# Spreading weight conversions over 19 steps, a longer output lag and one product on GpSimd, in a fused attention and gated MLP kernel

## The chip, the cores and the metric

The kernel runs on one core of one Trainium2 chip. The metric is the device time in microseconds, lower is better.

## The reference, cut to what matters

```python
# x: (8, 8, 512, 64), state: (8, 8, 32, 64); w_in: (512, 2048), w_out: (2048, 512), both float64
a  = softmax(scale * x @ state.T);  xread = a @ state        # tokens read the states
a2 = softmax(scale * state @ x.T);  sread = a2 @ x           # states read the tokens
t  = concat([xread, sread], axis=2)  -> (4352, 512)
h  = t @ w_in
return (h * cos(h)) @ w_out
```

The weights arrive as float64 and the kernel builds float32 from their bits on the chip. That is the conversion which the change moves.

## The kernel before

The kernel is one long software pipeline. Step s computes the hidden tile s (128 hidden features by 512 tokens of one batch), gates it, and multiplies a tile of some steps ago with `w_out`. Steps 0 to 15 are batch 0, steps 16 to 31 batch 1. The two form a pair with four phases of eight tiles (steps 0-7, 8-15, 16-23, 24-31), because the product with `w_out` is done in seven in place of eight block products; the sums of blocks s1 to s4 of `w_out` are built on GpSimd in steps 15 to 23.

A float64 piece of the weights is converted in parts on three engines:

```python
    def convert_part(i, p):
        ...
        if p == "1":   nc.scalar.activation(dst, raw_high, func=ACTF.Abs)
        elif p == "2": nc.scalar.activation(e, raw_low, func=ACTF.Copy, scale=2.0 ** -51, bias=2.0)
        elif p == "a": nc.vector.tensor_scalar(dst, dst, 2.0 ** -15, None, op0=ALU.max)          # L211
        elif p == "b": nc.vector.tensor_scalar(bits, bits, 3, None, op0=ALU.logical_shift_left)  # L213
        elif p == "c": nc.vector.scalar_tensor_tensor(...)                    # the sign, L216
        else:                                                                 # "d", L222
            engine = nc.vector if i == 1 else nc.gpsimd
            engine.tensor_tensor(bits, bits, e.bitcast(I32), op=ALU.add)      # the low word
```

There are 18 pieces for this pipeline. Pieces 0 to 3 are converted ahead of it (the last two parts of piece 3 in step 0). Piece i of the rest gets "1", "2", "a" and "b" at its step in `conv_at`, and "c" and "d" one step later. The order within a step, which is the order on each engine, is this (cut):

```python
    for step, t in enumerate(tiles()):
        ...
        hidden(t)            # TensorE: 2 x matmul of sw = w_in @ state with a, into one of two PSUM buffers
        go(0)                # TensorE work of the attention: products, token transposes, scores, ...
        gate(t)              # ScalarE copy + magic constant
        gate2(t)             # VectorE subtraction (first gate instruction on VectorE)
        go(1); go(3)         # ScalarE copies; VectorE copies, maxima, sums, norm1
        if last >= 0: convert(last, "cd")
        gate3(t)             # ScalarE Abs, Sin
        gate4(t)             # VectorE product h * cos(h): frees the PSUM buffer
        if conv >= 0: convert(conv, "1")                     # ahead of gate3 where go(1) is empty
        sums(t)              # differences of g for the block products (GpSimd in the first pair)
        go(2)
        if conv >= 0: convert(conv, "2")
        go(4)
        if conv >= 0: convert(conv, "ab")
        if step in block_at: blocks(*block_at[step])         # GpSimd
        while len(line) >= (LAG if step >= NH else LAG + 1): # LAG = 3, NH = 8
            output(line.pop(0))                              # TensorE: tile x w_out, L489
        line.append(t)
```

`norm1` is the product of the unnormalised attention with the spread inverse of its sums, 128x1024 float32 with both inputs in SBUF; for batch 1 it stands in step 11.

## Time and profile before

| | before |
|---|---|
| time, median | 821.85 us |
| TensorE busy / span | 765.5 / 819.9 us |
| TensorE's waits from 58 to 140 us | 17.4 us |
| ... after 140 us | 4.3 us |
| VectorE busy from 100 to 120 us | 17.99 of 20 us |

The table is read from the page's first part, from TensorE's waits by window and from the busy times by stretch; the prediction shows those lines.

### The profile page before, as it was taken

The numbers are of one execution on the slowest core, as the hardware profiler recorded it, in microseconds if no ns is written. First come the engines' busy times: TensorE is split into PE (matmuls) and PEld (weight loads), VectorE is DVE, ScalarE is ACT, GpSimd is POOL, SyncE is SP. The second block draws the span as 40 slices with busy tenths as digits, with TensorE's granted clock in tenths as the row PEclk, the third lists the DMA queues.
The fourth block names the chain that finished last, engine by engine and source line by source line (L and its number), as shares of the span: only waits on it lengthen the run. The fifth ranks groups of instructions, "written<-read, shape, count | busy, mean of one in ns | idle before, by whom it ended". The sixth has DMA issues, their size and how long they took to land.

```text
span 819.9 us, 7479 instructions
## 1 busy us (share of the span) xinstructions
PE 765.5 (93%) x2720; PEld 345.0 (42%) x2720; DVE 434.6 (53%) x672; ACT 397.9 (49%) x644; POOL 175.6 (21%) x117
## 2 busy tenths in 40 slices
PE   3569688989999999999999999999999999999997
PEld 2133233434444444444444444444344444455554
DVE  2799897653355435863454456743554355432431
ACT  2568675564447344644455454634473445322222
POOL 1134236877100000154000000451000002620200
PEclk9999999999999999999999999999999999999999
DMA  6574450102000211030010311120000112200021
GB/s 154 179 203 158 153 154 0 27 0 52 1 13 14 52 26 26 13 65 0 1 26 1 64 21 19 26 52 0 14 14 0 27 26 50 79 0 14 13 39 38
DMA packets 110500, 37.18 MB, mean 45 GB/s; under 512 B 102464, under 2 KB 102464, under 8 KB 110464
## 3 DMA queue, kind: packets, MB, share of 16 engines
q1 hardware_dynamic: 109248, 36.19, 18.8%
q10 hardware_dynamic: 1088, 0.26, 0.2%
q8 instruction: 21, 0.34, 0.2%
q0 software_dynamic: 128, 0.26, 0.2%
q14 instruction: 15, 0.12, 0.1%
HBM read 27.79 MB, written 8.91 MB: 45 GB/s over the span
## 4 chain that ended last, share of the span: by engine, by line
PE 78%; DVE 12%; ACT 7%; issue 1%; DMA 1%; POOL 0%; SPq 0%; DVEq 0%; POOLq 0%
PE o L489 42%; PE h L424 25%; PE at L276 4%; PE o L606 3%; DVE q L433 2%; PE at L363 2%; ACT q L439 1%; DVE g_all L445 1%; PE at L249 1%; ACT q L438 1%; DVE w_in L211 1%; DVE w_out L211 1%; DVE xT L296 1%; DVE aT L340 1%; DMA x_b<-in_x_dram 1%
## 5 line engine op out<-in xcount | busy, mean ns | idle before, releaser
L424 PE MATMUL h<-aT,sw 128*128 128x512 f32 x512 | 244.0, 599 | 17.9 <-DVE g_all L445 14.1
L489 PE MATMUL o<-g_all,w_out 128*128 128x512 f32 x512 | 236.5, 598 | 5.5 <-DVE sw L403 2.9
L430 ACT ACTIVATE q<-h 128x512 f32<-128x512 f32 (+1 forms) x144 | 82.2, 571 | 269.6 <-PE h L424 269.6
L451 POOL TENSOR_TENSOR g_all<-g_all 128x512 f32<-128x512 f32 x80 | 112.1, 1424 | 460.1 <-DVE g_all L445 454.5
L433 DVE SCALAR_TENSOR_TENSOR q<-q,h 128x512 f32<-128x512 f32 (+1 forms) x144 | 94.3, 655 | 208.0 <-ACT q L430 208.0
L489 PE MATMUL o<-g_all,s 128*128 128x512 f32 x384 | 177.3, 598 | 0.0
L445 DVE TENSOR_TENSOR g_all<-h,q 128x512 f32<-128x512 f32 (+1 forms) x144 | 94.8, 658 | 139.7 <-ACT q L439 139.4
L424 PEld LDWEIGHTS h<-aT,sw 128*128 128x128 f32 x512 | 96.6, 191 | 145.5 <-issue 109.3
L489 PEld LDWEIGHTS o<-g_all,w_out 128*128 128x128 f32 x512 | 93.6, 190 | 127.3 <-issue 119.8
L438 ACT ACTIVATE q<-q 128x512 f32<-128x512 f32 (+1 forms) x144 | 87.6, 608 | 103.6 <-DVE q L433 103.6
L489 PEld LDWEIGHTS o<-g_all,s 128*128 128x128 f32 x384 | 70.3, 190 | 88.4 <-issue 83.6
L439 ACT ACTIVATE q<-q,halfpi 128x512 f32<-128x512 f32 (+1 forms) x144 | 100.5, 698 | 4.5
L222 POOL TENSOR_TENSOR w_out<-w_out,s 128x1024 int32<-128x1024 int32 x10 | 23.8, 2385 | 87.5 <-DVE w_out L216 76.3
L451 DVE TENSOR_TENSOR g_all<-g_all 128x512 f32<-128x512 f32 x48 | 33.2, 692 | 1.6
L424 PE MATMUL h<-sT,w_in 128*128 128x256 f32 x128 | 30.2, 379 | 0.0
L405 ACT COPY sw<-at 128x512 f32<-128x512 f32 x48 | 25.7, 588 | 9.0 <-PE at L276 9.0
L606 PE MATMUL o<-w_out,g_all 128*128 128x512 f32 x64 | 29.6, 592 | 0.0
L222 POOL TENSOR_TENSOR w_in<-w_in,s 128x1024 int32<-128x1024 int32 (+1 forms) x9 | 18.0, 2000 | 53.8 <-DVE w_in L216 53.8
L424 PEld LDWEIGHTS h<-sT,w_in 128*128 128x128 f32 x128 | 24.3, 190 | 10.1 <-issue 6.7
L495 DVE SCALAR_TENSOR_TENSOR held<-o,held 128x512 f32<-128x512 f32 x40 | 25.5, 681 | 3.7 <-PE o L489 3.7
L276 PE MATMUL at<-w_in,stT 64*32 64x512 f32 x384 | 26.1, 601 | 0.0
L276 PE MATMUL o<-w_in,stT 64*32 64x512 f32 (+1 forms) x144 | 13.0, 606 | 13.3 <-POOL w_in L222 11.1
(79 smaller groups left out, 468.4 us busy)
## 6 DMA issues: line engine op xcount, KB each, us to landing
out_dram<-ot SPq DMA_DIRECT2D x136, 64.0 KB, 2.0
x_b<-in_x_dram SPq DMA_DIRECT2D x32, 256.0 KB, 4.5
g_all<-in_moe_w_out_dram SPq DMA_DIRECT2D x8, 1024.0 KB, 5.0
g_all<-in_moe_w_in_dram SPq DMA_DIRECT2D x6, 1024.0 KB, 5.3
g_all<-in_moe_w_in_dram SPq DMA_DIRECT2D x4, 512.0 KB, 7.0
x_b<-in_moe_w_out_dram SPq DMA_DIRECT2D x1, 1024.0 KB, 6.3
xT<-in_moe_w_out_dram SPq DMA_DIRECT2D x1, 1024.0 KB, 8.3
s<-in_state_dram ACTq DMA_DIRECT2D x4, 64.0 KB, 5.1
```

Source lines behind the costliest of these rows:

```text
L222: engine.tensor_tensor(bits, bits, e.bitcast(I32), op=ALU.add)
L276: nc.tensor.matmul(out=(to or at)[j][Ns * k:Ns * k + Ns, 0:n], lhsT=w[D * j:D * j + D, self.b, Ns * k:Ns * k + Ns], rhs=r(slice(D * j, D * ...
L405: nc.scalar.copy(dst, to[j][:, 0:c1 - c0])
L424: nc.tensor.matmul(out=t.hp, lhsT=t.lhs(i), rhs=t.rhs(i), start=(i == 0), stop=(i == t.kn - 1))
L430: nc.scalar.activation(t.q, t.hp, func=ACTF.Copy, bias=MAGIC)
L433: nc.vector.scalar_tensor_tensor(out=t.q, in0=t.q, scalar=MAGIC, in1=t.hp, op0=ALU.subtract, op1=ALU.subtract)
L438: nc.scalar.activation(t.q, t.q, func=ACTF.Abs)
L439: nc.scalar.activation(t.q, t.q, func=ACTF.Sin, bias=halfpi, scale=-TWO_PI)
L445: nc.vector.tensor_tensor(t.g, t.hp, t.q, op=ALU.mult)
L451: engine.tensor_tensor(out, a, b, op=ALU.subtract)
L489: nc.tensor.matmul(out=acc[bank][ch], lhsT=w[:, i, P * ch:P * ch + P], rhs=g.g, start=(i == 0), stop=(i == NH - 1))
L606: nc.tensor.matmul(out=acc[MAIN][i], lhsT=t.g[:, P * i:P * i + P], rhs=w_out[:, :, t.f, :], start=(n == 0), stop=(n == NF - 1))
```

## The change

Its intent is to give VectorE air in the first 16 steps: the 14 conversions are spread out to step 18, the outputs are held back one step longer through three phases so that weights and block sums may come later, and one attention product goes to GpSimd.

```diff
         def norm1(self):
-            nc.vector.tensor_tensor(self.aT, self.z1, self.spread, op=ALU.mult)
+            engine = nc.gpsimd if self.b == 1 else nc.vector
+            engine.tensor_tensor(self.aT, self.z1, self.spread, op=ALU.mult)
...
     conv_at = {s: 4 + i for i, s in enumerate(
-        (0, 1, 2, 3, 4, 5, 6, 7, 8, 10, 11, 12, 13, 14))}
+        (0, 1, 2, 3, 5, 6, 7, 8, 10, 12, 14, 15, 17, 18))}
...
-    block_at = {15: s1 lo, 17: s1 hi, 18: s2 lo, 19: s2 hi, 20: s4 lo, 21: s4 hi, 22: s3 lo, 23: s3 hi}
+    block_at = {16: s1 lo, 19: s1 hi, 20: s2 lo, 21: s2 hi, 22: s4 lo, 23: s4 hi, 24: s3 lo, 25: s3 hi}
...
-        while len(line) >= (LAG if step >= NH else LAG + 1):
+        while len(line) >= (LAG if step >= 3 * NH else LAG + 1):
```

(The operands of the block sums are unchanged and cut here.)

More of the change, by code (lines that the diff above doesn't have):

```diff
@@ L748 @@
     lo, hi = slice(0, NH // 2), slice(NH // 2, NH)
-    block_at = {15: (ALU.add, s1, a21, a22, lo),
-                17: (ALU.add, s1, a21, a22, hi),
-                18: (ALU.subtract, s2, s1, a11, lo),
-                19: (ALU.subtract, s2, s1, a11, hi),
-                20: (ALU.subtract, s4, a12, s2, lo),
-                21: (ALU.subtract, s4, a12, s2, hi),
-                22: (ALU.subtract, s3, a11, a21, lo),
-                23: (ALU.subtract, s3, a11, a21, hi)}
+    block_at = {16: (ALU.add, s1, a21, a22, lo),
+                19: (ALU.add, s1, a21, a22, hi),
+                20: (ALU.subtract, s2, s1, a11, lo),
+                21: (ALU.subtract, s2, s1, a11, hi),
+                22: (ALU.subtract, s4, a12, s2, lo),
+                23: (ALU.subtract, s4, a12, s2, hi),
+                24: (ALU.subtract, s3, a11, a21, lo),
+                25: (ALU.subtract, s3, a11, a21, hi)}
     LAG = 3
```

## The prediction

> **What bounds the kernel now.** I read the page's busy shares first, then the engines' busy time by stretch, then what TensorE waited for, then VectorE's and GpSimd's instructions in order of time. By stretch (us of the span; columns are length, then busy us and instructions of TensorE, its weight loads, VectorE, ScalarE, GpSimd; clock; DMA share; GB/s):
>
> ```profile
> PE 765.5 (93%) x2720; PEld 345.0 (42%) x2720; DVE 434.6 (53%) x672; ACT 397.9 (49%) x644; POOL 175.6 (21%) x117
> ...
> 80.00:100.00 20.00, 14.71 (x47) 5.48 (x46) 16.07 (x23) 12.48 (x18) 7.07 (x3) 1.00 0.45 157
> 100.00:120.00 20.00, 16.30 (x83) 6.93 (x81) 17.99 (x23) 15.27 (x23) 5.87 (x3) 1.00 0.39 131
> 120.00:140.00 20.00, 16.24 (x57) 7.00 (x58) 16.32 (x24) 12.32 (x20) 11.36 (x7) 1.00 0.12 28
> 140.00:160.00 20.00, 20.00 (x81) 8.38 (x80) 14.19 (x23) 10.49 (x17) 16.57 (x10) 1.00 0.17 28
> ...
> 240.00:280.00 40.00, 40.00 (x140) 18.08 (x140) 22.70 (x39) 21.56 (x34) 0.00 (x0) 1.00 0.18 33
> ```
>
> The reader sees two kernels. From 140 us on TensorE has work all the time (4.3 us of waits in 680 us). Before that VectorE is 80 to 95% busy and TensorE waits. The end is therefore the time at which TensorE becomes the bound, plus a tail of matmuls that the change does not shorten. Only TensorE's idle time before about 180 us can be won. From 58 us to 140 us it is this (TensorE's waits in that window):
>
> ```profile
> PE h L424 <- DVE g_all L445: 9.8, 7, 2.4
> PE o L489 <- DVE sw L403: 2.9, 1, 2.9
> PE o L489 <- POOL w_out L222: 2.6, 1, 2.6
> PE at L249 <- ACT xT L258: 1.9, 1, 1.9
> ```
>
> The hidden matmul of step s needs one of two PSUM buffers, so it waits for VectorE's last gate product of step s-2. After 140 us 2.83 us more go in steps 26 and 27 (at 170.9 and 176.5 us). Idle that could go: 9.8 + 2.9 + 1.9 + 2.8 = 17.4 us. The 2.6 us are at 58.8 us and hang on a conversion of step 3, which the change leaves.
>
> **Why VectorE is slow there.** Each conversion step has, on VectorE, "c" (the sign, 1.22 us) of the last piece, then "a" (maximum, L211) and "b" (shift, L213) of the next; GpSimd adds the low word (L222) once c is done. From VectorE's and GpSimd's order of time (start, us):
>
> ```profile
> 102.84 0.65 DVE L211 TENSOR_SCALAR w_out<-w_out 128x1024 f32<-128x1024 f32 x1
> ...
> 108.20 2.52 DVE L211 TENSOR_SCALAR w_out<-w_out 128x1024 f32<-128x1024 f32 x1
> ```
> ```profile
> 107.82 2.35 POOL L222 TENSOR_TENSOR w_out<-w_out,s 128x1024 int32<-128x1024 int32 x1 [12.33 <-DVE w_out L216]
> 113.32 2.38 POOL L222 TENSOR_TENSOR w_out<-w_out,s 128x1024 int32<-128x1024 int32 x1 [3.15 <-DVE w_out L216]
> ```
>
> The same "a" takes 0.65 us when GpSimd is idle (step 10, which follows a step without a conversion) and 2.52 us when it meets GpSimd's addition: it ends at 110.7, just after that addition at 110.2. In two neighbouring conversion steps this meeting is certain. In steps 4 to 14 the ten "a" take 1.71, 1.55, 1.68, 0.68, 1.34, 0.65, 2.52, 1.70, 1.29, 2.40 us, that is 9.0 us above ten times 0.65.
>
> [...] here 1024 elements take 0.65 us in "a" and 1.22 us in the attention product (L340)[...] here GpSimd takes 2.36 us for 128x1024 fp32 (L746) and VectorE 1.22, 1.93 times.
>
> **The change, part by part.**
>
> 1. Conversions at steps 0-3, 5-8, 10, 12, 14, 15, 17, 18 in place of 0-8 and 10-14. In steps 4 to 15 VectorE loses two a+b (2 x 1.3 = 2.6 us) and three c (11 to 8: 3 x 1.18 = 3.5 us). An "a" meets the addition only where the step before converted as well: steps 6, 7, 8 and 15 in place of 4-8 and 11-14. Of the 9.0 us of blocking I keep 1.0 + 0 + 0.7 (as steps 6 to 8 had) and 1.4 for step 15: 3.1, so 5.9 go. Sum 12.0 us of VectorE's path before step 16.
>
> 2. Given back: steps 16 to 19 get two a+b, three c and one or two blocked "a", 2.6 + 3.5 + 1.5 = 7.6 us. The gates (1.3 us a step), a copy and an evacuation there are about 8.5 us, so 16.1 us of VectorE beside four steps of TensorE work (132.5 to 149.3, 16.8 us). It just fits, hence mostly hidden, with VectorE able to stall TensorE by a microsecond or two.
>
> 3. The attention product of the second batch goes to GpSimd: 1.22 us off VectorE in step 11, 2.36 us onto GpSimd, idle from 95.5 to 107.8. Its result is needed at step 16. But it becomes ready as "a" and "b" of step 10 start and can block one of them by up to 2.4 us. I book 0 net.
>
> 4. The lag of four keeps one more output waiting through steps 8 to 23. No matmul is added. One output pair (4 x 0.43 = 1.72 us) leaves step 8 and comes back in step 24, just ahead of the wait of 1.86 us at step 26, which it fills. Its use is slack: a22, a21 and the sums of blocks may be later by a step. The late blocks fit: GpSimd's last additions end about step 19, the s1 half needed at step 24 likewise, s4 by step 23, needed at step 27.
>
> Step by step from VectorE's first gate subtraction (start before, estimate after, from the durations above): step 5 65.5, 63.1; step 8 84.5, 81.1; step 10 97.5, 94.1; step 12 111.4, 104.5; step 14 122.4, 113; step 16 132.3, 123.5. The gain of 8.8 us is less than the 12.0 of part 1, since steps 9 and 10 are held by ScalarE's exponentials with two table loads (1.28 us each, 93.3 to 100.3), and steps without a conversion still need the chain hidden, copy, subtraction, Abs, Sin, product or 3.4 to 5.5 us of TensorE. TensorE then becomes the bound at step 17 or 18, some 9 us earlier than now. I take off about 1 us for part 2 and for small operations of the third batch's softmax (sums at step 24) that GpSimd's later blocks can now hold up: 168.7 us falls now into a pause of GpSimd of 4.0 us, which the late blocks fill. Gain 8 us: 821.8 - 8.0 = 813.8.
>
> **Rivals.**
> A. TensorE takes over as soon as VectorE is relieved, all 17.4 us but a few go: about 806. For it: TensorE is busy 17.95 of 20 us already at 60 to 80. Against it: the exponentials of step 9 and VectorE's chain in steps 10 to 13 remain.
> B. The wait moves to the weights. Pieces 8 and 11 are converted a step later, but their products stay at steps 7 and 10. Today the addition of piece 11 ends at 89.98 and its product starts at 90.05, no slack at all. I expect waits of TensorE for GpSimd of 1 us at step 7 and up to 3 us at step 10; the latter in place of the 2.9 us wait for sw, as the chain through the exponentials ends no earlier. If they add to it instead: about 817.
> C. GpSimd becomes the bound in steps 16 to 25: with additions, differences and blocks it is busy nearly without pause (step 19: 2.36 + 1.28 + 2.36 = 6.0 us against 4.4 us of TensorE). [...] the gain shrinks to 2 to 4 us: about 818. Against: TensorE reads GpSimd's results four steps later.
> D. Nothing moves, as VectorE's sum is only shifted: ruled out by step 16 to 25 having TensorE full and VectorE at 70% now.
>
> **Range and chances.** Central 813.8, from 809 (A in part) to 818.5 (B or C). A gain of over 2% needs 16.4 us of the 17.4 that exist, so 0.03; a loss of over 2% would need a new wait of 25 us, 0.01; within 2%, 0.96.
>
> **What would show it.** Part 1: "a" of about 0.65 us in steps 5, 10, 12, 14; TensorE's wait for the gate product from 58 to 140 us down from 9.8 to 3 to 5 us. Part 3: no VectorE attention product in step 11, one of 2.4 us on GpSimd, and a "b" or "c" of over 2 us beside it. Part 4: two outputs at step 24, the wait at step 26 near zero. B: TensorE waits for GpSimd's w_in at steps 7 and 10. C: TensorE waiting for GpSimd's g_all or s, or for VectorE in steps 17 to 25, by over 3 us. The busy time of TensorE should stay at about 765 us. I am wrong if its idle time before 180 us doesn't fall by 6 to 10 us, or if idle appears after 180 us.

## More of the kernel before

The kernel before takes 821.85 us (median of 6 runs, 821.24 to 821.96); in later rounds, on several chips, its medians were 821.2 to 822.0 us. Each later round ran it again, so a ratio compares a kernel with the kernel before of its own rounds.

TensorE of the kernel before has almost no waits after about 140 us, so what a change wins or loses shows in the time at which a given step's hidden matmul starts.

## The result, and the profile after

The changed kernel takes 828.63 us (median of 6 runs, 827.57 to 829.22). The ratio is 1.0083, 95% interval 1.007 to 1.0096. A ratio is the mean time of the one kernel's fast runs over the mean of the other's fast runs of the same rounds, so not quite the ratio of the medians. It is slower by 0.8%, where 1% faster had been expected.

Every line number below `norm1` is one higher than before. TensorE's waits of the changed kernel from 58 to 140 us (us in total, times, longest):

```profile
PE o L490 <- POOL w_out L222: 9.6, 3, 4.6
PE o L276 <- POOL w_in L222: 4.8, 2, 4.1
PE h L425 <- DVE g_all L446: 0.2, 1, 0.2
```

The waits for VectorE's gate product did go, from 9.8 to 0.2 us. In their place TensorE waits 14.4 us for the last part of a weight piece, GpSimd's addition of the low word; only 2.6 us of these, at 58 us, were there before. After 140 us there are new waits as well, where before had only those for the gate product:

```profile
PE h L425 <- DVE g_all L446: 3.5, 3, 2.1
PE at L249 <- ACT xT L258: 3.0, 1, 3.0
PE o L276 <- DVE held L496: 1.3, 1, 1.3
```

The second is a token transpose in step 19 that waits until ScalarE, in step 18, has copied the PSUM bank that it writes; the third is the product in step 20, which needs a PSUM bank that VectorE has not yet emptied. The longest wait for a weight piece, and the matmuls behind it, stand in step 12:

```profile
108.87 3.78 PE L490 MATMUL o<-g_all,w_out 128*128 128x512 f32 x4 [4.60 <-POOL w_out L222]
112.45 2.61 PE L425 MATMUL h<-aT,sw 128*128 128x512 f32 x4
```

Four such matmuls take 1.88 to 1.98 us in most other steps. The trace's granted clock was 0.50 from 108.87 to 112.45 us, 0.71 from there to 115.00 and 1.00 from 115 to 117. Such slow records after a wait are called the slow clock below.

Where the time goes is read best from the start of the hidden matmuls (us; from the instructions in order of time):

| step | before | changed | difference |
|---|---|---|---|
| 12 | 101.82 | 101.51 | -0.3 |
| 13 | 108.33 | 112.45 | +4.1 |
| 17 | 132.48 | 131.70 | -0.8 |
| 19 | 140.33 | 139.87 | -0.5 |
| 20 | 144.64 | 148.81 | +4.2 |
| 21 | 149.29 | 155.44 | +6.2 |
| 24 | 160.81 | 166.95 | +6.1 |
| 25 | 164.24 | 172.10 | +7.9 |
| 27 | 176.46 | 183.69 | +7.2 |
| 28 | 182.94 | 190.17 | +7.2 |

So there are two things to explain: why nothing was won by step 19, and why 6.6 us are lost in steps 19 and 20, with some 1 us more by step 28.

For the second, VectorE of the changed kernel in steps 17 and 18, in order of time (start, us; L211 is "a", L213 "b", L216 "c"):

```profile
138.05 0.85 DVE L211 TENSOR_SCALAR w_out<-w_out 128x1024 f32<-128x1024 f32 x1
138.94 2.72 DVE L213 TENSOR_SCALAR w_out<-w_out 128x1024 int32<-128x1024 int32 x1
...
142.18 1.70 DVE L216 SCALAR_TENSOR_TENSOR w_out<-g_all,w_out 128x1024 int32<-128x1024 int32 x1
...
144.74 2.20 DVE L211 TENSOR_SCALAR w_out<-w_out 128x1024 f32<-128x1024 f32 x1 [0.26 <-ACT w_out L205]
146.98 1.64 DVE L213 TENSOR_SCALAR w_out<-w_out 128x1024 int32<-128x1024 int32 x1
```

And GpSimd beside it (L747 is the first half of the block sum s1, L452 the differences of tiles):

```profile
138.31 2.81 POOL L747 TENSOR_TENSOR s<-w_out 128x1024 f32<-128x1024 f32 x1
141.07 1.72 POOL L452 TENSOR_TENSOR g_all<-g_all 128x512 f32<-128x512 f32 x1
144.02 2.37 POOL L222 TENSOR_TENSOR w_out<-w_out,s 128x1024 int32<-128x1024 int32 x1 [1.23 <-DVE w_out L216]
146.35 1.72 POOL L452 TENSOR_TENSOR g_all<-g_all 128x512 f32<-128x512 f32 x1
```

"b" takes 0.69 us when free; here it starts inside the block sum and ends 0.5 us after it, at 141.66 against 141.12. "c" then meets the tile's difference, "a" the low word, the second "b" the next difference. The excess over the free times 0.65, 0.69, 1.22, 0.65 and 0.69 us is 0.20 + 2.03 + 0.48 + 1.55 + 0.95 = 5.2 us. The way from there to TensorE goes over ScalarE, in step 18, and ends at the transpose of step 19 (L440 is the Sin, L205 part "1" of the next piece, L258 the token copy):

```profile
142.29 0.63 ACT L439 ACTIVATE q<-q 128x512 f32<-128x512 f32 x1 [2.86 <-DVE q L434]
142.95 0.72 ACT L440 ACTIVATE q<-q,halfpi 128x512 f32<-128x512 f32 x1
143.58 1.13 ACT L205 ACTIVATE w_out<-g_all 128x1024 f32<-128x1024 f32 x1
144.62 0.56 ACT L258 COPY xT<-at 128x512 f32<-128x512 f32 x1
```
```profile
145.23 1.11 PE L249 MATMUL at<-ident,x_b 128*128 128x128 f32 x4 [3.05 <-ACT xT L258]
```

ScalarE waits 2.86 us for VectorE's gate subtraction, which "b" held up; about 1 us more of TensorE's wait is the next piece's part "1", which stands ahead of the copy.

### The profile page after: what moved, and what is told of

It is laid out like the page before. It is cut to its first block, busy times and chain, and to the rows that moved or that the text cites. A ratio compares the mean times of both kernels' runs of the same rounds, so it can differ in the third digit from the quotient of the medians.

```text
span 827.4 us, 7476 instructions
## 1 busy us (share of the span) xinstructions
PE 771.6 (93%) x2720; PEld 348.3 (42%) x2720; DVE 436.1 (53%) x671; ACT 397.9 (48%) x644; POOL 180.3 (22%) x118
## 4 chain that ended last, share of the span: by engine, by line
PE 78%; DVE 10%; ACT 8%; issue 2%; DMA 1%; POOL 1%; SPq 0%; DVEq 0%; POOLq 0%
PE o L490 42%; PE h L425 25%; PE at L276 4%; PE o L607 3%; PE at L364 2%; DVE q L434 2%; ACT q L440 1%; ACT q L439 1%; DVE g_all L446 1%; PE at L249 1%; DVE xT L296 1%; DVE aT L341 1%; DMA x_b<-in_x_dram 1%; DVE w_out L211 1%; ACT q L431 1%
## 5 line engine op out<-in xcount | busy, mean ns | idle before, releaser
L490 PE MATMUL o<-g_all,w_out 128*128 128x512 f32 x512 | 240.7, 607 | 9.6 <-POOL w_out L222 9.6
L452 POOL TENSOR_TENSOR g_all<-g_all 128x512 f32<-128x512 f32 x80 | 114.0, 1448 | 453.6 <-DVE g_all L446 449.6
L440 ACT ACTIVATE q<-q,halfpi 128x512 f32<-128x512 f32 (+1 forms) x144 | 100.5, 698 | 4.5
L276 PE MATMUL o<-w_in,stT 64*32 64x512 f32 (+1 forms) x144 | 16.5, 631 | 19.5 <-POOL w_in L222 16.0
L452 DVE TENSOR_TENSOR g_all<-g_all 128x512 f32<-128x512 f32 x48 | 33.2, 692 | 1.6
```

Source lines behind the costliest of these rows:

```text
L276: nc.tensor.matmul(out=(to or at)[j][Ns * k:Ns * k + Ns, 0:n], lhsT=w[D * j:D * j + D, self.b, Ns * k:Ns * k + Ns], rhs=r(slice(D * j, D * ...
L440: nc.scalar.activation(t.q, t.q, func=ACTF.Sin, bias=halfpi, scale=-TWO_PI)
L452: engine.tensor_tensor(out, a, b, op=ALU.subtract)
L490: nc.tensor.matmul(out=acc[bank][ch], lhsT=w[:, i, P * ch:P * ch + P], rhs=g.g, start=(i == 0), stop=(i == NH - 1))
```

## The experiments

All kernels but the two marked as wrong gave the right result. "Lost" times are differences of the hidden matmul's start, read as in the table above.

### The parts alone

n_pool is before with the `norm1` part of the diff alone, l_lag with the last line alone, c_conv with the two tables alone, cl with all but `norm1`.

> The kernel before with only the attention product of the second batch on GpSimd. Theory T1 (the loss comes from long waits of TensorE for late weight pieces and from the slow clock that follows such a wait): the product blocks one VectorE shift (b) of step 10 by about 2 us and saves 1.2 us in step 11, no wait of TensorE over 3 us arises, so 0 to +1.5 us, ratio 1.000 to 1.002. Rival T2 (the product on GpSimd is what costs): +4 us or more, ratio over 1.005.

Measured: 822.78 us, ratio 1.0016 (1.0002 to 1.003). The time is as T1 has it; against it, one wait of 3.26 us for a gate product did arise, in step 13. The block is seen on VectorE and on GpSimd in step 10:

```profile
102.06 0.65 DVE L211 TENSOR_SCALAR w_out<-w_out 128x1024 f32<-128x1024 f32 x1
102.74 2.74 DVE L213 TENSOR_SCALAR w_out<-w_out 128x1024 int32<-128x1024 int32 x1
```
```profile
102.28 2.66 POOL L341 TENSOR_TENSOR aT<-aT,xT 128x1024 f32<-128x1024 f32 x1 [7.55 <-ACT q L431]
```

The product comes in between "a" and "b", and "b" waits for its end: 2.05 us lost for 1.22 us saved.

> The kernel before with only the lag of four up to step 23. T1: a pair of output matmuls (1.72 us) moves from step 8 to step 24, where it fills the 1.86 us wait; the wait for sw at step 11 (2.9 us) can shrink; time within 1.5 us of before, ratio 0.998 to 1.002. Rival T3 (the lag costs, since it leaves TensorE without work in step 8 and evacuates the SIDE bank a step later, into the product of step 20): +2 to +4 us.

Measured: 822.41 us, ratio 1.0004 (0.9992 to 1.0017). The lag alone costs nothing that these rounds can tell.

> The kernel before with only the 19-step spread (conversion and block steps), lag as before. T1: the output of tile 8 comes at step 11, the very step in which piece 12's low word is added, so TensorE waits there 5 to 7 us with a slow clock after it: slower than the full change, ratio 1.008 to 1.014 (828.5 to 833 us), granted clock about 0.975. T2 or T3 (product or lag cost): faster than the full change by 3 us or more, ratio under 1.005.

Measured: 830.73 us, ratio 1.0109 (1.0096 to 1.0123), in the expected range; TensorE's wait at step 11 was longer than expected, with slow matmuls behind it (four of them take 3.78 us in place of 1.88):

```profile
108.02 3.78 PE L489 MATMUL o<-g_all,w_out 128*128 128x512 f32 x4 [9.99 <-POOL w_out L222]
```

So the schedule of the conversions is the part that costs, and the longer lag softens it: the output of tile 8 stands one step later.

> The full change without the product on GpSimd. T1: piece 12 is ready about 0.9 us earlier (the 2.7 us shift of step 10 falls back to 0.7, the product costs 1.1 in step 11), the wait at step 12 falls from 4.6 to about 3.7 us, the rest stays: 826 to 828.5 us, ratio 1.005 to 1.008. T2: back to 822 us or below.

Measured: 828.27 us, ratio 1.0081 (1.0067 to 1.0095). The product on GpSimd explains none of the loss within these intervals (828.63 with it, 828.27 without). T2 and T3 are out. The wait at step 12 did not fall, though: it is 4.96 us in this profile, as TensorE, too, came to it earlier.

### Early or late: each half undone

d1_early_back is the full change with pieces 4 to 12 where they were:

```diff
-        (0, 1, 2, 3, 5, 6, 7, 8, 10, 12, 14, 15, 17, 18))}
+        (0, 1, 2, 3, 4, 5, 6, 7, 8, 12, 14, 15, 17, 18))}
```

> The full change with pieces 4 to 12 converted at steps 0 to 8 again (as before) and pieces 13 to 17 at 12, 14, 15, 17, 18 (as in the change). Theory T1': two separate places: early, late pieces 8, 9, 11 and 12 make TensorE wait, and late, GpSimd blocks VectorE in steps 17 and 18 so that ScalarE copies the tokens late and TensorE loses some 6.7 us in steps 19 and 20. Here the waits for w_in and w_out between 64 and 130 us vanish (9.6 + 4.8 us to about 3), TensorE reaches the hidden matmul of step 19 some 3 to 5 us earlier than in the full change, and the loss at steps 19 and 20 stays: 823 to 827 us, ratio 1.002 to 1.006. Rival (the late weight pieces are all of it): at or below 819 us.

Measured: 823.79 us, ratio 1.0024 (1.001 to 1.0037), as T1' has it, 4.8 us below the full change. TensorE's waits from 58 to 130 us of this kernel:

```profile
PE h L425 <- DVE g_all L446: 5.6, 3, 3.0
PE o L490 <- POOL w_out L222: 2.6, 1, 2.6
```

The waits for weights that the change had added are gone (the 2.6 us one was there before). The hidden matmul of step 19 starts at 132.65 us, 7.7 us earlier than before and 7.2 us earlier than in the full change (3 to 5 had been expected). So the relief that had been predicted exists. But step 20 starts at 141.91 and step 21 at 148.20: of the 7.7 us, 6.6 are lost in two steps, and at step 28 nothing is left (182.93 against 182.94). The profiled run is the fastest of the five, 822.00 us, 1.8 us under their median; e1_no_pool and e2_no_conv below, which differ from this kernel only in step 16 and later but for a constant written once at the start, reach step 19 at 134.82 and 134.03 us. The lead at step 19 is therefore better given as 5.5 to 7.7 us. The same four meetings of VectorE and GpSimd are there, "b" of step 17 with 2.72 us again.

d2_late_back keeps the early half and converts pieces 13 to 17 at steps 11 to 15, with the block table of before:

```diff
-        (0, 1, 2, 3, 5, 6, 7, 8, 10, 12, 14, 15, 17, 18))}
+        (0, 1, 2, 3, 5, 6, 7, 8, 10, 11, 12, 13, 14, 15))}
-    block_at = {16: s1 lo, 19: s1 hi, 20: s2 lo, ...
+    block_at = {15: s1 lo, 17: s1 hi, 18: s2 lo, ...
```

> The full change with pieces 13 to 17 at steps 11 to 15 and the block sums at their old steps, so that no conversion lies in steps 16 to 19 but the sign of piece 17; pieces 4 to 12 stay late. T1': the wait of 3.0 us for the token copy at step 19 and the 1.3 us wait for held go, the waits for w_in and w_out stay: 822 to 826 us, ratio 1.001 to 1.005. Rival (late weight pieces are all of it): no faster than the full change, 828 us or more.

Measured: 827.83 us, ratio 1.0083 (1.0066 to 1.0099). The two waits of steps 19 and 20 did go, yet the time stayed, so the expectation missed. The rival's sentence is all but met in number, but the trace shows another reason: step 15 now has a conversion beside the first half of s1, its "b" takes 2.72 us, and TensorE waits 4.6 us for the gate product in step 18. The loss had moved two steps forward. This run alone does not tell the theories apart.

late_v is the full change with the low words of pieces 15 to 17 on VectorE and the first half of s1 at step 18:

```diff
-            engine = nc.vector if i == 1 else nc.gpsimd
+            engine = nc.vector if i in (1, 15, 16, 17) else nc.gpsimd
-    block_at = {16: (ALU.add, s1, a21, a22, lo),
+    block_at = {18: (ALU.add, s1, a21, a22, lo),
```

> The full change with GpSimd kept off VectorE's way in steps 16 to 19: the low words of pieces 15, 16 and 17 added on VectorE (0.69 us each) and the first half of the block sum s1 moved from step 16 to 18. T1': the shift of step 17 falls from 2.7 to 0.7 us, the sign and maximum of step 18 lose their blocking (5.2 us in all), the waits at steps 19 and 20 (3.0 and 1.3 us) fall to under 1.5 us together: 822 to 825 us. Rival (VectorE's added work itself, not the blocking, makes the token copy late): within 1 us of the full change.

Measured: 831.84 us, ratio 1.0125 (1.0107 to 1.0143): slower than the full change, both theories missed. The low word of a whole piece takes 1.23 us on VectorE, not the 0.69 us of a half piece (128x512, in the kernel before) that I had taken, and the moved sum met the sign of piece 17:

```profile
145.99 2.78 DVE L216 SCALAR_TENSOR_TENSOR w_out<-g_all,w_out 128x1024 int32<-128x1024 int32 x1
148.80 1.22 DVE L222 CUSTOM_DVE_ANT_0 w_out<-w_out,s 128x2048 uint16<-128x2048 uint16 x1
```

It left VectorE no pause from 136.6 to 152.4 us, and the wait of step 20 for the bank grew to 4.0 us. A sound attempt had to take something away without putting anything in.

### The slow clock

f_fill repeats matmuls that write the same values again, inside the three longest waits of the full change:

```diff
         def tokens(self, k):
-            for c in range(NC): ...
+            for _ in range(7 if (self.b, k) == (2, 2) else 1): for c in range(NC): ...   # step 19
         def turn(self, j):
+            for _ in range(6 if (self.b, j) == (1, 1) else 1): ...                        # step 12
         # products of batch 0, column block 3: [0, 1] three more times ahead of [0, 1, 2, 3], step 10
```

> The full change with repeated matmuls (same result written again) put into the three longest waits of TensorE: three repeats of the ready half of the product at step 10, five repeats of one transposed head at step 12, six repeats of a token transpose at step 19; some 6 us of extra work, so that no wait there is over 2.5 us. T1': the slow clock after those waits costs time only where TensorE stays the bound after it, that is at step 19, so -1 to -2 us against the full change (826.5 to 827.5). Rival (the slow clock is the cause, its 6.1 us of extra TensorE busy time being the loss): -4 to -6 us, 823 to 824.5.

Measured: 829.84 us, ratio 1.0095 (1.008 to 1.0109). It gained nothing, against the rival's 4 to 6 us and also against my 1 to 2. The filling did what it should in step 12: the output after it, four matmuls, took 1.98 us after a wait of 3.69 us, in place of 3.78 us. (That wait was to stay under 2.5 us; it did not.) In step 20, where the wait for the bank grew to 2.64 us, the slow matmuls came back (four output matmuls took 3.67 us). In the profiled runs f_fill starts the hidden matmul of step 19 3.0 us ahead of the full change (136.92 against 139.87) and loses 8.3 us in steps 19 and 20 in place of 6.6. The kernel before speaks against the clock as well: in one set of rounds its runs had mean granted clocks from 0.979 to 0.997, and those two took 821.48 and 821.95 us. I read TensorE's extra 6.1 us of busy time (771.6 in the changed kernel, 765.5 before) as mostly a slower filling of time in which it would have waited; this is not shown, and a part of it may cost at steps 19 and 20, which no run here separates.

### No conversion after step 15

d4_by15 is d1_early_back with pieces 13 to 17 at 10, 12, 13, 14, 15; d5_by15_dve has the attention product on VectorE again on top of that. Against the full change:

```diff
-        (0, 1, 2, 3, 5, 6, 7, 8, 10, 12, 14, 15, 17, 18))}
+        (0, 1, 2, 3, 4, 5, 6, 7, 8, 10, 12, 13, 14, 15))}
-            engine = nc.gpsimd if self.b == 1 else nc.vector    # d5_by15_dve only
+            engine = nc.vector
```

> As the kernel with the early pieces back (pieces 4 to 12 at steps 0 to 8), but pieces 13 to 17 at 10, 12, 13, 14, 15, so that none is converted after step 15; block sums, lag and the product on GpSimd as in the change. T1': no wait for the token copy (3.0 us) or for held at steps 19 and 20, and no late weight pieces: TensorE waits only for gate products; below before, 816 to 821 us, ratio 0.993 to 0.999. Rival (the lag and the later block sums make the late loss, not the conversions of steps 17 and 18): the loss at steps 19 to 28 stays, 823 us or more.

Measured: 825.16 us, ratio 1.0044 (1.0032 to 1.0057). Missed. The number is in the rival's range, but 2.7 us are lost by step 19 already (143.02 against 140.33), ahead of where the rival puts the loss. The waits of steps 19 and 20 are gone, but VectorE has the same number of conversions ahead of step 16 as before, the last four of them one step later: its first gate subtraction of step 16 comes at 133.26 us against 132.34, the sign of piece 17 stands ahead of that step's gate product (136.19 against 134.47), and the hidden matmul of step 18 waits for it. A gap by itself gives nothing if the same work has to be done by the same step.

> The same with the attention product of the second batch on VectorE again. If the product on GpSimd blocks VectorE's shift of step 10 (2.0 us) for 1.2 us saved, this is 0 to 2 us faster than d4_by15; if it pays, slower by 1 us or more.

Measured: 825.88 us, ratio 1.0045 (1.0032 to 1.0057): no difference from d4_by15.

### What makes the late loss

T4 puts the late loss down to the VectorE instructions that GpSimd holds up, such as the "b" of step 17 (2.72 us, 0.69 free). e1_no_pool is d1_early_back without the first half of s1 and without GpSimd's differences of steps 16 to 19. Its output is wrong, which doesn't matter for the time.

```diff
-        if t.phase == 2:
+        if t.phase == 2 and (pr.n or i >= 4):
-        if step in block_at:
+        if step in block_at and step != 16:
```

> Wrong result on purpose. As d1_early_back (823.8 us), but GpSimd's first half of the block sum s1 (step 16) and its differences of steps 16 to 19 are left out, so that beside VectorE's conversions of steps 17 and 18 only the low words' additions remain. Theory T4[...]: the shift of step 17 falls from 2.7 to 0.7 us, the loss of 6.6 us at steps 19 and 20 falls to under 3 us: 819 to 821 us. Rival T5 (the conversions' own work on VectorE and ScalarE in steps 16 to 19 makes the loss): within 1 us of 823.8.

Measured: 819.98 us, ratio 0.9975 (0.9961 to 0.9988), in T4's range and 3.8 us below d1_early_back. The same five instructions, step 17 and 18:

```profile
133.00 0.68 DVE L211 TENSOR_SCALAR w_out<-w_out 128x1024 f32<-128x1024 f32 x1
133.72 0.70 DVE L213 TENSOR_SCALAR w_out<-w_out 128x1024 int32<-128x1024 int32 x1
...
134.92 1.22 DVE L216 SCALAR_TENSOR_TENSOR w_out<-g_all,w_out 128x1024 int32<-128x1024 int32 x1
...
137.52 1.70 DVE L211 TENSOR_SCALAR w_out<-w_out 128x1024 f32<-128x1024 f32 x1 [0.37 <-ACT w_out L205]
139.25 0.69 DVE L213 TENSOR_SCALAR w_out<-w_out 128x1024 int32<-128x1024 int32 x1
```

Only the meeting with the low word's addition is left (1.70 us). This run takes away blocking and adds nothing, so GpSimd's hold on VectorE is shown as a cause of the late loss. The 3.8 us are a difference of medians from rounds on two chips; the two ratios to before differ by 0.0049, or 4.0 us.

e2_no_conv, wrong too, is d1_early_back with pieces 16 and 17 not converted:

```diff
     def convert_part(i, p):
+        if i in (16, 17):
+            return
...
+    for i in (16, 17):            # once, at the start
+        nc.gpsimd.memset(loads[i][0], 0.01)
```

> Wrong result on purpose. As d1_early_back, but the two pieces of steps 17 and 18 are not converted at all (their place is filled with a constant at the start), GpSimd's sums and differences stay. T4 and T5 both expect the loss at steps 19 and 20 to go: the 7 to 8 us that d1_early_back is ahead of before at step 19 then reach the end, less 1 us at step 26: 814.5 to 817 us. If another cause (lag, later sums) makes the loss: 821 us or more.

Measured: 817.70 us, ratio 0.9952 (0.9939 to 0.9965), just above the range. The hidden matmul of step 21 is 5.8 us ahead of before and that of step 28 still 4.7 us. So the lag and the later block sums take about 1 us between steps 21 and 28, and the two late conversions with what they meet cost 6.1 us: 3.8 us through GpSimd's other work, the other 2.3 us, if the two add, their own work on VectorE and ScalarE and their low words, which no run takes apart.

### Versions that follow from it

v_early is the kernel before with the low words of pieces 2 to 6 on VectorE; d6_both is d5_by15_dve with the same line:

```diff
-            engine = nc.vector if i == 1 else nc.gpsimd
+            engine = nc.vector if 1 <= i <= 6 else nc.gpsimd
```

> The kernel before with the low words of pieces 2 to 6 added on VectorE (1.2 us each there, 0.7 for the half pieces) in place of GpSimd (2.36 us), so that the maximum of the next piece is not blocked in steps 1 to 3 (1.5 to 1.75 us each) and pieces 5 and 6 are ready sooner (TensorE waits 3.6 and 2.6 us for them). If GpSimd's exclusive hold and the late piece set the pace there: 2 to 4 us faster, 818 to 820. If VectorE's own load does: no faster.

Measured: 819.91 us, ratio 0.9974 (0.996 to 0.9987), as expected: the "a" of steps 1 to 3 take 0.68 us each, where before had 2.37, 2.14 and 2.40.

> d5_by15_dve and v_early together. If the gains are in separate stretches (steps 0 to 3, steps 9 to 19) they add: the sum of both within 1 us.

Measured: 823.17 us, ratio 1.0017 (1.0005 to 1.003). The gain of v_early came on top of d5_by15_dve's loss, as expected: 825.88 - 823.17 = 2.7 us.

b1_one_late has pieces 4 to 12 at steps 0 to 8 and the rest at 10, 12, 14, 15, 17, so only one after step 15, with lag and later sums of the change and the product on VectorE. b2_best adds v_early's line and moves the last block sum s3 from steps 24 and 25 to 29 and 30. Against the full change, beside `norm1` on VectorE:

```diff
-        (0, 1, 2, 3, 5, 6, 7, 8, 10, 12, 14, 15, 17, 18))}
+        (0, 1, 2, 3, 4, 5, 6, 7, 8, 10, 12, 14, 15, 17))}
-                24: s3 lo, 25: s3 hi          # b2_best
+                29: s3 lo, 30: s3 hi
```

> Pieces 4 to 12 at steps 0 to 8, 13 to 17 at 10, 12, 14, 15, 17, lag of four, later sums, product on VectorE. Only one piece is converted after step 15, so VectorE has less to do in steps 16 to 19 than in d1_early_back by one a+b and one c, and it is relieved before: 816 to 820 us if the loss there grows with the number of pieces; 823 or more if a single late piece suffices for it.

Measured: 821.23 us, ratio 0.9995 (0.9982 to 1.0007): between the two branches, level with before. Its "b" of step 17 still takes 2.72 us.

> b1_one_late with the low words of pieces 2 to 6 on VectorE (2 us faster alone) and the last block sum at steps 29 and 30 in place of 24 and 25, away from the attention product of step 25 (3.2 us there against 2.1 before): 2 to 3 us faster than b1_one_late.

Measured: 817.76 us, ratio 0.995 (0.9937 to 0.9964), 3.5 us below b1_one_late, a little more than expected. With s3 moved, the wait of step 27 is 0.98 us again, in place of 2.06 in b1_one_late.

b3_sum_later is b2_best with one GpSimd instruction moved:

```diff
-    block_at = {16: (ALU.add, s1, a21, a22, lo),
+    block_at = {18: (ALU.add, s1, a21, a22, lo),
```

> b2_best with the first half of the block sum s1 at step 18 in place of 16, behind the last low word, so that GpSimd is not at it while VectorE shifts piece 17 in step 17 (2.72 us there, 0.69 free) and no later conversion is met: the wait of 2.2 us for the token copy at step 19 goes to under 1 us. If the sum is done before the output of step 20 needs it: 1 to 2.5 us faster than b2_best, 815.3 to 816.8; if it is late, TensorE waits for s there and nothing is won.

Measured: 815.68 us, ratio 0.9933 (0.9919 to 0.9946), the fastest kernel. The "b" of step 17 takes 1.64 us, since a tile's difference still meets it:

```profile
131.75 1.64 DVE L213 TENSOR_SCALAR w_out<-w_out 128x1024 int32<-128x1024 int32 x1
```

The wait for the token copy at step 19 fell from 2.2 to 1.1 us, a little short of the expectation, the time came as expected by the medians (2.1 us below b2_best); by the ratios it is 1.4 us, and their intervals overlap. What late_v had spoiled with the same move was that a sign of the next piece and two low words stood there on VectorE; here no further conversion follows.

## Why the prediction was wrong

**What bounds the kernel.** Right: only TensorE's idle time ahead of step 28 moved, and the stretch after step 28 was the same to 0.4 us. (VectorE's "80 to 95%" are 80 to 91% in the stretches of 20 us.) Rival A is out: TensorE's waits from 58 to 140 us fell from 17.4 to 14.6 us only.

**Part 1, relief of VectorE.** The sum was right and its way to the end was not. The blocking of "a" in steps 5 to 15 is 3.2 us above the free time, 3.1 had been booked, and step by step as booked (1.06, 0.68 and 1.32 us in steps 6, 8 and 15). Only "this meeting is certain" is too strong: in step 7 "a" was not held (0.68 us, before and after). With the early pieces back, step 19 started 5.5 to 7.7 us earlier, against the "some 9 us" predicted. The step that failed is the chain from VectorE to TensorE, which took every weight piece but 8 and 11 to be ready in time. VectorE's first subtraction was put at 94.1, 113 and 123.5 us in steps 10, 14 and 16 and came at 95.83, 121.40 and 131.59 (before: 97.51, 122.41, 132.34): in steps 13 and 14 VectorE itself waited 3.31 and 2.15 us for hidden matmuls that came late behind the output of step 12, whose weights were not ready. With as many conversions ahead of step 16 but no added wait for weights, in d1_early_back, e2_no_conv and e1_no_pool, it came at 114.11 to 116.34 us in step 14 and at 124.38 to 126.54 in step 16: within 3.4 us of the estimate, in place of 8.

**Rival B.** It named the right wait, with its sizes for those two (0.7 and 4.1 us measured, 1 and up to 3 predicted), and it missed pieces 9 and 12: at step 8 TensorE waited 2.4 us for piece 9, needed by the output of tile 4, and at step 12 4.6 us for piece 12, needed by tile 8. Converted two steps later with one step of lag, piece 12 lost the slack that it had. The alternative "in place of the 2.9 us wait" came true for step 10: no wait for sw is left, and step 12 starts 0.3 us earlier than before. The wait for piece 12 behind it was not in the sum.

**Part 2, what is given back.** The mis-sized term is the blocking in steps 16 to 19: 1.5 us booked, 5.2 us measured. I had counted meetings of "a" with one addition; in truth GpSimd had its instructions back to back there, so "b" (2.72 and 1.64 us, 0.69 free) and the sign (1.70 us, 1.22 free) were held as well. "It just fits" became 6.6 us lost in steps 19 and 20. The path is VectorE's gate subtraction late, ScalarE's Abs and Sin late, the next piece's part "1" (1.13 us) and the token copy behind them late, TensorE idle. Rival C had GpSimd busy nearly without pause there and the gain down to 2 to 4 us, without the size of the loss.

**Part 3, the product on GpSimd.** The block was foreseen (up to 2.4 us; 2.0 measured); 0 net had been booked, alone it costs 1.3 us by its ratio of 1.0016.

**Part 4, the lag.** Right as a cost: 1.0004 alone, and the wait of step 26 was filled. The wait of step 27 was missed: beside GpSimd's block sum in step 25 the attention product on VectorE takes 3.18 us, 2.10 before (1.22 free), so that wait grew from 0.97 to 2.06 us.

**The sum.** 8 us had been expected as gain, from some 9 us by step 18. The profiled runs give: 5.5 to 7.7 us by step 19 if no weight is late, of which the full change kept 0.5; then minus 6.6 us at steps 19 and 20, and about minus 1 us up to step 28. By these numbers either fault alone was enough to take the gain.

**Still open.** How much of the 4.6 us at step 12 and of the loss in steps 19 and 20 goes through the slow clock was not isolated. f_fill speaks against it being the whole: step 12 was free of slow matmuls and nothing was won, but in step 20 there still were some. The two tables of the change, conversions and block sums, were also never run one without the other.

## What to carry to other kernels

Before moving work later in a pipeline of several engines, list for each moved item the step that needs it on every engine, not only on the one that is relieved; a relieved engine can end up waiting for the engine that now lacks its input, as VectorE did here for 3.31 and 2.15 us in steps 13 and 14. Where a trace shows one engine's instruction running on until another engine's ends, as "b" did beside GpSimd's block sum (2.72 us, 0.69 free), count the back-to-back instructions of the one beside each instruction of the other: here each of five VectorE instructions of two steps was held, for 0.2 to 2.0 us. Test such a cause by taking work away, with a wrong result if need be: the two attempts here that moved work into the gap only moved the collision.

## What the traces show of held instructions, slow matmuls and the low word

- In the kernel before, from 63 to 129 us, eight of the ten "a" met GpSimd's addition and took 1.29 to 2.52 us (0.65 free); each ended 0.54 to 0.56 us after the addition. In the changed kernel GpSimd's block sum started during the "a" of step 17, which passed in 0.85 us; the "b" right behind it, started within the block sum, took 2.72 (0.69 free). The block sum took 2.81 us there, 2.35 to 2.37 in the kernel before.
- In the changed kernel four output matmuls took 3.78 us after a wait of 4.60 us (1.88 to 1.98 in most other steps) and four took 2.59 us after a wait of 2.66 us; in n_pool four hidden ones took 3.68 us after 2.32 us. But four took 1.98 us after a wait of 3.69 us in f_fill, and 1.95 us after 2.90 us in the kernel before, so the length of the wait did not by itself tell what followed. Two runs of the kernel before had mean granted clocks of 0.979 and 0.997 and took 821.48 and 821.95 us.
- The int32 addition of the low word of a whole piece ran on VectorE as a custom operation on 128x2048 uint16, with the right result (late_v, v_early), in 1.23 us against 2.35 us on GpSimd.
